# Key places by chunk, shared query places, and later planned sums in a scheduled attention and FNet kernel

## The chip, the cores and the metric

The kernel runs on one core of a Trainium2 chip. Five engines work beside each other: TensorE (matmuls), VectorE (DVE), ScalarE (ACT), GpSimd (POOL) and SyncE (SP), which in this kernel issues every DMA. Each engine takes its instructions strictly in the order in which the program has them. The metric is the device time of one execution in microseconds, the median of several runs.

## The reference

Two independent halves are computed in float32, and written side by side into an output of 2048 x 896.

```python
# A: Fourier mixing, x of 2048 x 448
a = einsum("bsd,ed->bse", x, dft_hid_re); b = einsum("bsd,ed->bse", x, dft_hid_im)
y = einsum("ts,bse->bte", dft_seq_re, a) - einsum("ts,bse->bte", dft_seq_im, b)
# B: softmax attention, 16 heads of width 28 over 2048 tokens
q, k, v = split(x @ wqkv)
p = softmax(q k^T * 28 ** -0.5)
out = (p v) @ wo
```

The inputs of B are multiplied by 8, so that the scores are large and the softmax needs its row maxima.

## The kernel before, in words

**Accuracy.** Products that need more than one pass are split into a high and a low part ("hi", "lo"): three passes for the products of `products`, and for the scores 84 rows of a key or query tile (28 of one part twice, 28 of the other).

**Half A and the projections** are "filling" work for TensorE: the projection of queries, keys and values (L547), the hidden transform (`hidden`, also L547), and the transform along the sequence (`sequence`, L662, 1536 matmuls of 448 columns). Their weights come through three buffers "wraw" (DMA at L515), are rounded by ScalarE (L516), and POOL takes the rest (L522). Query and key parts are written to a DRAM tensor "qkd" and loaded from there, per head and chunk.

**Attention** is cut into units of one head and one chunk of 512 queries, 64 in all, in two lanes. A "kept" unit (`unit_kept`, 48 of them) scores once: 16 matmuls (L803) with keys as rows, copies kept in SBUF (L415), a running maximum on VectorE (L810, L813), the maximum turned and spread by transposes (L820, L822, L829, L831), then the shift on POOL or VectorE (L846), the exponential on ScalarE (L850), and the product with the values (L734). A "twice" unit (`unit_twice`, 16) scores once for the maxima alone (L753, L757), sends the 4 x 128 maxima through DRAM into two more rows of its query tile (L765 to L770, tensor "nmd"), and scores again with these rows (L781), so that ScalarE's exponential (L785) reads the shifted scores at once. Each head has one twice unit, mostly the chunk 1.

**The sums** (`out_of`, L854 to L884): once per head (per chunk for the last two heads) TensorE folds the four partial results (L865), ScalarE copies them (L867), a DMA gathers the rows of sums into a small tile "sm" (L870), VectorE inverts them (L871), they go to DRAM (L872, "rd") and come back spread over 32 partitions (L876), POOL multiplies (L879), and the result is stored (L882). At the end the output projection loads it again (L939, L944), splits it into halves hi and lo that stand in a key tile (L956, L411), and multiplies by wo (L974).

**What sets the order.** Nothing is ordered by hand. All work is given to a planner (`Schedule`) as tasks, each with an engine, a key (when it is due), an estimated duration, dependencies, and the buffer places that it uses. The planner plays through an estimated course: whenever an engine is free, it takes the ready task with the smallest key for which places are free, and emits it. So the estimates fix each engine's order once and for all; on the chip an engine that comes to an instruction whose input is late waits, and everything behind it on that engine waits too. For a DMA the estimate is the size, plus the `extra` microseconds given in the call, and SP is taken as busy for 0.38 us per DMA.

**Places.** A pool of places (`Slots`) gives them out when a task that uses one is emitted, and takes one back when its last user is done. With `in_turn` a place goes only to the earliest due takers. A head's keys are one place of 128 x 2048, of two (`kt_s`); `head_loads` fills it with four chunk loads of two DMAs each (L689, L690), due one microsecond after the other. Twice units take one of two query places "qr", kept units one of two "qk".

Of the kernel before, what the change touches and what calls it, by code (L numbers as in the profile page):

```python
# [20 lines left out]
S = 2048  # L21
D = 448
H = 16
DH = 28
# [10 lines left out]
LATE = 110.0  # L35
NFILL = 2
# [280 lines left out]
def tile_kernel(ctx, tc, xa, wre, wim, wd, xb, wqkv, wo, out):  # L317
# [381 lines left out]
    def head_loads(h):  # L699
        k = KT[h] = kt_s.slot()  # L700
        for c in range(NC):
            got_k[h, c] = [dma(head_due[h] - 14 + c, lambda c=c: rows_of(
                k.t[:, c * CH:(c + 1) * CH], 1, h * 2 * DH + DH, c * CH, (c + 1) * CH),
                size=84, extra=X_ROWS, n=2, deps=rows_ready(h, c, DH), use=[k])]
        v = VT[h] = v_s.slot()
        got_v[h] = [dma(head_due_b[h] - 12, lambda: nc.sync.dma_start(
            v.t.rearrange("p c t d -> p (c t d)"), v_d[h]), deps=[d for c in range(NC) for d in v_done[c]], use=[v])]
# [34 lines left out]
    def unit_twice(u):  # L742
        h, c = u
        t_a, t_b, dt = due[u]
        q = qr_s.slot()
# [3 lines left out]
        for kc in range(NC):  # L749
            for qt in range(4):  # L750
                o = bank_s.slot()
                key = t_a + (kc * 4 + qt) * dt
                m = pe(key, lambda e, o=o, kc=kc, qt=qt: nc.tensor.matmul(  # L753
                    o.t, q.t[:KR, qt * P:(qt + 1) * P], KT[h].t[:KR, kc * CH:(kc + 1) * CH], start=True, stop=True),
                    deps=[*lq, *got_k[h, kc], before.get("ra")], use=[o, q, KT[h], mx])
# [17 lines left out]
        for g in range(NT // GV):  # L773
            tiles, es = [], []
            for kt in range(GV * g, GV * (g + 1)):
                o = bank_s.slot()
                if kt % 2 == 0:
                    tiles.append(kept_s.slot())
                p = Half(tiles[-1], kt % 2)
                key = t_b + kt * dt  # L780
                m = pe(key, lambda e, o=o, kt=kt: nc.tensor.matmul(  # L781
                    o.t, KT[h].t[:KR + 2, kt * P:(kt + 1) * P], q.t[:KR + 2, :], start=True, stop=True),
                    deps=[ld, before.get("rb")], use=[o, p.pair, q, KT[h], po])
                in_line("rb", m)
                es.append(act(key - 20, lambda o=o, p=p: nc.scalar.activation(p.t, o.t, AF.Exp, scale=SCALE),  # L785
                              deps=[m], use=[o, p.pair]))
            last_pv = pv_group(u, g, tiles, [*es, last_pv], po, key)
        unit_out(u, po, last_pv, key - 20)

    def unit_kept(u):  # L790
        h, c = u
        t_a, t_b, dt = due[u]
        q = qk_s.slot()
# [3 lines left out]
        for kt in range(NT):  # L797
            o = bank_s.slot()
            if kt % 2 == 0:
# [4 lines left out]
                o.t, KT[h].t[:KR, kt * P:(kt + 1) * P], q.t[:KR, :], start=True, stop=True),  # L804
                deps=[*lq, *got_k[h, kt // 4], before.get("ka")], use=[o, s.pair, rm, q, KT[h]])
# [50 lines left out]
    def out_of(us, rd):  # L856
# [13 lines left out]
        s2 = dma(key, lambda: nc.sync.dma_start(sm.t[:, :n * NC], osb.t[DH:n * VW:VW, :]), 8, 0.7, deps=[a], use=[sm, pair])  # L870
        r = dve(key - 20, lambda: nc.vector.reciprocal(sm.t[:, :n * NC], sm.t[:, :n * NC]), 0.3, deps=[s2], use=[sm])  # L871
        s3 = dma(key, lambda: nc.sync.dma_start(rd, sm.t[:, :n * NC]), 8, deps=[r], use=[sm])  # L872
# [5 lines left out]
        s4 = dma(key, spread, 64, n=n, deps=[s3], use=[pair])  # L878
# [52 lines left out]
    for n, c in enumerate(LAST):  # L931
# [15 lines left out]
        for i in range(2):  # L947
            x = kt_s.slot()
            ready = []
            for k in range(4):  # L950
                raw, ld = raws[k]
                src = lambda raw=raw, i=i: raw.t[:, i * HF:(i + 1) * HF]
                hi = lambda x=x, k=k: x.t[:, k * HF:(k + 1) * HF]
                lo = lambda x=x, k=k: x.t[:, (4 + k) * HF:(5 + k) * HF]
                key = T_OUT + n + i / 2
                a = act(key, lambda hi=hi, src=src: nc.scalar.activation(hi(), src(), AF.Copy), 0.3, deps=[ld], use=[raw.pair, x])  # L956
                if k < 3:
                    b = sub(key, lo, src, lambda hi=hi: f32(hi()), d=0.35 if OUT_DVE else 0.65, early=OUT_DVE, deps=[a], use=[raw.pair, x])
                else:
                    b = sub(key, lambda hi=hi: hi()[64:], lambda src=src: src()[64:], lambda hi=hi: f32(hi())[64:], d=0.35 if OUT_DVE else 0.65, early=OUT_DVE,  # L960
                            deps=[a], use=[raw.pair, x])
                ready += [a, b]
            for t in range(2):
                o = bank_s.slot()

                def cols(k, x=x, t=t):
                    return lambda: x.t[:, k * HF + t * P:k * HF + (t + 1) * P]
# [7 lines left out]
                m = pe(key, emit, n=11, d=M448, deps=[*ready, *wo_ready], use=[o, x])  # L975
# [44 lines left out]
```

## Time and profile before

| what | value |
|---|---|
| runs (3) | 1185.16, 1185.59 and 1194.47 us, median 1185.59 |
| profiled execution, own time | 1186.24 us |
| its span, first to last instruction | 1184.5 us |
| mean granted clock of TensorE | 0.997 |
| busy: ACT | 89% |
| busy: DVE | 79% |
| DMA, mean rate over the span | 106 GB/s |

The span is the time between the first and the last instruction in the trace; the execution's own time has 1.7 us around it. "Busy" counts computing instructions of an engine. The trace also tells, for each idle piece of an engine, which other engine or DMA ended it ("<-"), and the chain of waits follows the end of the program back from releaser to releaser. "SPq" is SP's queue: what it shows as a duration is the issue of a DMA, not its transfer.

### The profile page before, as it was taken

How to read it: one execution, taken by the hardware profiler on the slowest of the kernel's cores; microseconds unless marked ns; L12 is line 12 of the kernel's file. 1: busy time of each engine (PE TensorE's matmuls, PEld its weight loads, DVE VectorE, ACT ScalarE, POOL GpSimd, SP SyncE). 2: the span in 40 equal slices, each digit the busy share in tenths (PEclk: the TensorE clock that was granted, in tenths of full speed). 3: DMA queues.
4: the chain of work that ended last, by engine and by line, in shares of the span. 5: the costliest groups of instructions: out<-in, count | busy, mean ns of one | idle time of the engine just before them, and what ended most of it. 6: DMA issues, size and time to landing. Idle time of an engine off the chain costs nothing.

```text
span 1184.5 us, 19835 instructions
## 1 busy us (share of the span) xinstructions
PE 1164.1 (98%) x6426; PEld 809.4 (68%) x6426; DVE 936.7 (79%) x1468; ACT 1056.5 (89%) x1777; POOL 909.9 (77%) x525
## 2 busy tenths in 40 slices
PE   8999999999999999999999999999999999999998
PEld 7876656666667666766666667666667676667677
DVE  6599988888888868877787888987877888877742
ACT  5279999999999989998899999999999999999942
POOL 1157868989888979877797989897987897997730
PEclk9999999999999999999999999999999999999999
DMA  7792235322323232323132232323232423223643
GB/s 244 165 225 107 100 124 174 90 81 62 106 68 110 62 109 67 105 72 90 62 102 89 78 118 67 106 64 111 83 99 89 121 76 115 87 62 100 188 130 119
DMA packets 111736, 125.18 MB, mean 106 GB/s; under 512 B 49264, under 2 KB 63216, under 8 KB 111632
## 3 DMA queue, kind: packets, MB, share of 16 engines
q1 hardware_dynamic: 111632, 123.91, 35.4%
q8 instruction: 51, 0.84, 0.3%
q14 instruction: 53, 0.43, 0.1%
HBM read 89.98 MB, written 33.75 MB: 104 GB/s over the span
## 4 chain that ended last, share of the span: by engine, by line
PE 82%; ACT 6%; DMA 4%; DVE 2%; issue 2%; POOL 2%; SPq 1%; ACTq 0%; POOLq 0%; DVEq 0%
PE bank L662 23%; PE bank L734 17%; PE bank L803 14%; PE bank L547 11%; PE bank L781 5%; PE bank L753 5%; PE bank L974 3%; ACT kept L415 3%; PE bank L820 2%; PE bank L829 2%; DVE rm L813 2%; ACT kept L850 1%; PE bank L865 1%; DMA kept<-xb 1%; POOL kept L846 1%
## 5 line engine op out<-in xcount | busy, mean ns | idle before, releaser
L846 POOL TENSOR_TENSOR kept<-kept,mb 128x1024 f32<-128x1024 f32 x263 | 626.9, 2404 | 124.0 <-ACT mb L831 101.4
L813 DVE TENSOR_TENSOR rm<-bank,rm 128x512 f32<-128x512 f32 x672 | 461.1, 686 | 74.9 <-ACT kept L415 33.5
L415 ACT ACTIVATE kept<-bank 128x512 f32<-128x512 f32 (+1 forms) x715 | 408.5, 633 | 53.9 <-PE bank L803 34.6
L850 ACT ACTIVATE kept<-kept 128x1024 f32<-128x1024 f32 x372 | 395.1, 1102 | 11.3 <-DVE kept L846 5.5
L662 PE MATMUL bank<-big,whi 128*128 128x448 f32 x1024 | 328.6, 370 | 0.0
L803 PE MATMUL bank<-qk,k 84*128 84x512 f32 x768 | 292.0, 410 | 2.7 <-ACT kept L415 1.4
L522 POOL TENSOR_TENSOR wlo<-wraw,whi 128x512 fp32r<-128x512 f32 (+1 forms) x166 | 204.0, 1232 | 70.3 <-ACT whi L516 46.7
L734 PE MATMUL bank<-kept,v 128*32 128x512 f32 x1988 | 240.7, 597 | 0.7 <-DVE rm L813 0.5
L662 PEld LDWEIGHTS bank<-big,whi 128*128 128x128 f32 x1024 | 193.7, 190 | 28.8 <-issue 3.5
L803 PEld LDWEIGHTS bank<-qk,k 84*128 84x128 f32 x768 | 141.9, 189 | 69.3 <-DVE rm L813 17.7
L662 PE MATMUL bank<-big,wlo 128*128 128x448 f32 x512 | 189.0, 369 | 0.0
L757 DVE TENSOR_REDUCE mx<-bank 128x1 f32<-128x512 f32 x256 | 173.3, 682 | 18.8 <-PE bank L753 18.0
L785 ACT ACTIVATE kept<-bank 128x512 f32<-128x512 f32 x250 | 157.6, 639 | 5.3 <-PE bank L781 5.0
L734 PEld LDWEIGHTS bank<-kept,v 128*32 128x32 f32 x1988 | 56.6, 109 | 124.0 <-issue 111.9
L846 DVE TENSOR_TENSOR kept<-kept,bank 128x1024 f32<-128x1024 f32 x109 | 131.8, 1212 | 2.6 <-ACT mb L831 2.4
L516 ACT ACTIVATE whi<-wraw 128x512 fp32r<-128x512 f32 x167 | 112.1, 673 | 17.0 <-DMA wraw<-wqkv 12.2
L781 PE MATMUL bank<-qr,k 86*128 86x512 f32 x256 | 104.3, 411 | 2.9 <-DMA qr<-nmd 2.2
L662 PEld LDWEIGHTS bank<-big,wlo 128*128 128x128 f32 x512 | 97.2, 190 | 13.7 <-issue 0.8
L753 PE MATMUL bank<-k,qr 84*128 84x512 f32 x256 | 103.5, 413 | 2.3 <-ACT kept L785 0.9
L547 PE MATMUL bank<-wd,whi 128*128 128x448 f32 x256 | 80.6, 368 | 0.1
L547 PE MATMUL bank<-big,whi 128*128 128x512 f32 x196 | 69.8, 400 | 2.0 <-ACT big L482 0.9
L822 DVE TENSOR_REDUCE nm<-bank 128x4 f32<-128x512 f32 x48 | 33.1, 690 | 46.5 <-PE bank L820 43.4
(80 smaller groups left out, 1062.0 us busy)
## 6 DMA issues: line engine op xcount, KB each, us to landing
wraw<-wre SPq DMA_DIRECT2D x64, 256.0 KB
wraw<-wim SPq DMA_DIRECT2D x64, 256.0 KB
qkd<-wd SPq DMA_DIRECT2D x32, 256.0 KB
wraw<-xa SPq DMA_DIRECT2D x32, 256.0 KB
k<-qkd SPq DMA_DIRECT2D x64, 112.0 KB
out<-kept SPq DMA_DIRECT2D x32, 224.0 KB
qkd<-kept SPq DMA_DIRECT2D x24, 256.0 KB
qk<-qkd SPq DMA_DIRECT2D x48, 112.0 KB
```

Of the source, the lines that this page charges most:

```text
L415: nc.scalar.activation(dst, src, AF.Copy)
L522: b = sch.add(e, at, lambda g: eng[g].tensor_tensor(self.lo.t[:, :n], raw.t[:, :n], f32(self.hi.t)[:, :n], op=ALU.subtract), deps=[a], acq ...
L547: nc.tensor.matmul(o.t[:, :cols], w(), x(), start=(i == 0), stop=(i == n - 1))
L662: nc.tensor.matmul(o.t[:, :D], a.t[:, k, :], b[:, q * 4 + k, :], start=(q == 0 and k == 0 and j == 0), stop=(q == 3 and k == 3 and j == 2))
L734: nc.tensor.matmul(o.t[j * VW:(j + 1) * VW, :], VT[h].t[:, kt // 4, j, :], pairs[i // 2].t[:, i % 2, :], start=(kt < 4), stop=(kt >= NT - 4))
L753: m = pe(key, lambda e, o=o, kc=kc, qt=qt: nc.tensor.matmul(o.t, q.t[:KR, qt * P:(qt + 1) * P], KT[h].t[:KR, kc * CH:(kc + 1) * CH], start ...
L757: ms.append(dve(key - 20, lambda o=o, kc=kc, qt=qt: nc.vector.tensor_reduce(mx.t[:, qt, kc:kc + 1], o.t, axis=AX.X, op=ALU.max), deps=[m], ...
L781: m = pe(key, lambda e, o=o, kt=kt: nc.tensor.matmul(o.t, KT[h].t[:KR + 2, kt * P:(kt + 1) * P], q.t[:KR + 2, :], start=True, stop=True), ...
L803: m = pe(key, lambda e, o=o, kt=kt: nc.tensor.matmul(o.t, KT[h].t[:KR, kt * P:(kt + 1) * P], q.t[:KR, :], start=True, stop=True), deps=[*l ...
L813: prev = dve(key - 20, lambda o=o: nc.vector.tensor_tensor(rm.t, o.t, rm.t, op=ALU.max), deps=[m, prev], use=[rm, o], lock=[o], own=RAW)
L846: eng[e].tensor_tensor(s.t, s.t, over_pair(pm.t if e == "DVE" else mb.t), op=ALU.add)
L850: es.append(act(key, lambda s=s: nc.scalar.activation(s.t, s.t, AF.Exp, scale=SCALE), 0.96, deps=[sh], use=[s]))
```

## The change

Three things are changed.

1. A head's keys are no longer one tile of 128 x 2048 of two, but four tiles of 128 x 512 of eight (`NKEYS = 8`); the memory is the same. Each chunk's tile is taken by its own load and given back after its own last matmul. The matmuls read the chunk's tile. The output projection takes four such tiles for its halves where it took one large tile.
2. The two pools of two query places become one pool of four, given out in the order of need to both lanes.
3. In `out_of` the planner's estimate of three DMAs rises: the gathering of the sums by 3.0 instead of 0.7 us, the store of the reciprocals and their spreading by 1.5 us each instead of nothing. No instruction changes through this; the planner puts what depends on them later.

```diff
+NKEYS = 8
-    kt_s = new("k", [P, S], F32R, 2, True)
+    kt_s = new("k", [P, CH], F32R, NKEYS, True)
-    qk_s = new("qk", [P, CH], F32R, 2, True)
-    qr_s = new("qr", [P, CH], F32R, 2, True)
+    q_s = new("q", [P, CH], F32R, 4, True)
...
     def head_loads(h):
-        k = KT[h] = kt_s.slot()
+        KT[h] = [kt_s.slot() for c in range(NC)]
         for c in range(NC):
-            got_k[h, c] = [dma(head_due[h] - 14 + c, lambda c=c: rows_of(
-                k.t[:, c * CH:(c + 1) * CH], 1, h * 2 * DH + DH, c * CH, (c + 1) * CH),
+            k = KT[h][c]
+            got_k[h, c] = [dma(head_due[h] - 14 + c, lambda k=k, c=c: rows_of(
+                k.t, 1, h * 2 * DH + DH, c * CH, (c + 1) * CH),
                 size=84, extra=X_ROWS, n=2, deps=rows_ready(h, c, DH), use=[k])]
...
-                    o.t, KT[h].t[:KR, kt * P:(kt + 1) * P], q.t[:KR, :], start=True, stop=True),
-                deps=[*lq, *got_k[h, kt // 4], before.get("ka")], use=[o, s.pair, rm, q, KT[h]])
+                    o.t, KT[h][kt // 4].t[:KR, kt % 4 * P:(kt % 4 + 1) * P], q.t[:KR, :], start=True, stop=True),
+                deps=[*lq, *got_k[h, kt // 4], before.get("ka")], use=[o, s.pair, rm, q, KT[h][kt // 4]])
...
-        s2 = dma(key, lambda: nc.sync.dma_start(sm.t[:, :n * NC], osb.t[DH:n * VW:VW, :]), 8, 0.7, deps=[a], use=[sm, pair])
+        s2 = dma(key, lambda: nc.sync.dma_start(sm.t[:, :n * NC], osb.t[DH:n * VW:VW, :]), 8, 3.0, deps=[a], use=[sm, pair])
...
-        s3 = dma(key, lambda: nc.sync.dma_start(rd, sm.t[:, :n * NC]), 8, deps=[r], use=[sm])
+        s3 = dma(key, lambda: nc.sync.dma_start(rd, sm.t[:, :n * NC]), 8, 1.5, deps=[r], use=[sm])
...
-        s4 = dma(key, spread, 64, n=n, deps=[s3], use=[pair])
+        s4 = dma(key, spread, 64, 1.5, n=n, deps=[s3], use=[pair])
...
-            x = kt_s.slot()
+            x = [kt_s.slot() for _ in range(4)]
...
+                xh, xl = x[k // 2], x[2 + k // 2]
```

The same replacement of `KT[h]` by the chunk's tile stands in the two scoring passes of `unit_twice`, and `q_s.slot()` in both unit functions. At the start POOL fills rows 64 to 95 of every key tile with ones (L374); these are now eight tiles.

More of the change, by code (lines that the diff above doesn't have):

```diff
@@ L744, in unit_twice @@
         t_a, t_b, dt = due[u]
-        q = qr_s.slot()
+        q = q_s.slot()
         lq = load_q(u, q)
@@ L781, in unit_twice @@
                 m = pe(key, lambda e, o=o, kt=kt: nc.tensor.matmul(
-                    o.t, KT[h].t[:KR + 2, kt * P:(kt + 1) * P], q.t[:KR + 2, :], start=True, stop=True),
-                    deps=[ld, before.get("rb")], use=[o, p.pair, q, KT[h], po])
+                    o.t, KT[h][kt // 4].t[:KR + 2, kt % 4 * P:(kt % 4 + 1) * P], q.t[:KR + 2, :], start=True, stop=True),
+                    deps=[ld, before.get("rb")], use=[o, p.pair, q, KT[h][kt // 4], po])
                 in_line("rb", m)
@@ L792, in unit_kept @@
         t_a, t_b, dt = due[u]
-        q = qk_s.slot()
+        q = q_s.slot()
         lq = load_q(u, q)
@@ L974, in emit @@
                         nc.tensor.matmul(o.t[:, :D], x(), w(), start=(n == 0), stop=(n == 10))
-                m = pe(key, emit, n=11, d=M448, deps=[*ready, *wo_ready], use=[o, x])
+                m = pe(key, emit, n=11, d=M448, deps=[*ready, *wo_ready], use=[o, *x])
                 pair = kept_s.slot()
```

16 lines of the change are left out of this document (8 added, 8 removed).

## The prediction

> **What bounds the kernel now.** I read the page's first two parts for the bounding engine, then the waits of TensorE alone, then the chain of waits around each of them, and last the SP queue's timeline at the worst one.
>
> ```profile
> span 1184.5 us, 19835 instructions
> PE 1164.1 (98%) x6426; PEld 809.4 (68%) x6426; DVE 936.7 (79%) x1468; ACT 1056.5 (89%) x1777; POOL 909.9 (77%) x525
> ```
>
> TensorE is busy for 1164.1 of 1184.5 us, so its idle time is 20.4 us. A change that adds and removes no matmul can win little more than this, and only the part that it touches.
>
> ```profile
> PE bank L781 <- DMA qr<-nmd: 2.2, 3, 0.8
> PE bank L829 <- DVE nm L822: 1.9, 1, 1.9
> PE bank L803 <- ACT kept L415: 1.4, 1, 1.4
> PE bank L753 <- ACT kept L785: 0.9, 1, 0.9
> PE bank L803 <- ACT ou L415: 0.8, 1, 0.8
> PE bank L753 <- DVE rm L813: 0.7, 1, 0.7
> PE bank L781 <- DVE rm L810: 0.6, 1, 0.6
> PE bank L753 <- DMA qr<-qkd: 0.6, 1, 0.6
> PE bank L734 <- DVE rm L813: 0.5, 1, 0.5
> PE bank L803 <- ACT kept L785: 0.2, 1, 0.2
> ```
>
> These are TensorE's own waits in the attention part (total us, times, longest), ten rows with 9.8 us in all; the rest of its idle time lies at the start, where both programs have the same order, at the end, and in pieces too short for this view. The chain of waits shows what stands ahead of most of them:
>
> ```profile
> 172.30 2.30 DMA sm<-kept
> 416.14 1.43 DMA qr<-nmd
> 422.06 4.30 DMA sm<-kept
> 552.50 2.54 DMA sm<-kept
> 624.94 2.17 DMA kept<-rd
> 681.85 2.91 DMA wraw<-wd
> 932.22 1.46 DMA qr<-nmd
> ```
>
> "sm" and "rd" belong to a head's sums and reciprocals (out_of), "nmd" to the row maxima of the twice lane (the first and the last of three such waits), "wraw" to a weight load. All are small or single transfers on the SP queue. What stands ahead of them there is shown by the SP timeline at the worst place:
>
> ```profile
> 548.26 0.60 ACT L867 ACTIVATE kept<-bank 128x512 f32<-128x512 f32 x1 [0.30 <-PE bank L865]
> 546.78 0.80 SPq L689 DMA_DIRECT2D k<-qkd  x1
> 547.62 0.54 SPq L690 DMA_DIRECT2D k<-qkd  x1
> ...
> 552.05 0.35 SPq L706 DMA_DIRECT2D v<-vd  x1
> 552.50 0.61 SPq L870 DMA_DIRECT2D sm<-kept  x1
> 555.07 0.25 DVE L871 RECIPROCAL sm<-sm 128x16 f32<-128x16 f32 x1 [4.13 <-DMA sm<-kept]
> ```
>
> The first row is ScalarE's copy of the sums, ready at 548.9. A head's whole key tile comes free at once, so its four chunks (0.80 + 0.54 us of issue each), a query load and the values go out in one burst from 546.8 to 552.4. The sums' transfer L870 stands behind it. VectorE has the reciprocal next in its order and idles for 4.13 us; TensorE waits 0.6 (L753, for the query load in the burst) and 1.9 us (L829, for the maximum behind the reciprocal). The order of SP in the program has such a burst at every head: between two chunk loads of one head stand mostly 0 or 2 other issues, and L870 or L769 follows. The same burst delays the maxima at the three places and the weight load at 681.85.
>
> ```profile
> 553.60:557.20 3.60, 1.69 (x10) 1.03 (x9) 2.13 (x5) 0.59 (x2) 0.00 (x0) 1.00 0.39 117
> 557.20:560.60 3.40, 3.40 (x11) 2.89 (x10) 3.20 (x5) 3.07 (x6) 2.39 (x1) 0.50 0.47 137
> ```
>
> These windows show that the granted clock (the column behind POOL) is 0.50 for the 3.4 us after this wait. At half clock that stretch does 1.7 us of work, so 1.7 us more are lost.
>
> **The change, part by part.**
>
> *Work.* The two built orders hold the same matmuls: 5329 TensorE instructions in each, and 220 switches between 32-column and full-width matmuls in each. The first 679 stand in the same order. So TensorE's busy time stays, and the prediction is a matter of its waits.
>
> *Keys in eight places.* Chunk loads stay 128 DMAs of the same size. In the new SP order, however, 4 to 8 other rows stand between two chunk loads of a head, so the burst is gone. One chunk (1.4 us of issue) can still stand ahead of L870 or L769. This takes away the three waits on nmd (2.2), the wait on the query load (0.6) and the one that follows the weight load at 681.85 (L753 behind L785, 0.9): 3.7 us. New is that each chunk load waits for its own place on SP; behind it stand weight loads. I bound this in the rivals.
>
> *Queries in four shared places.* No instruction changes. The twice lane's first scoring pass now begins earlier: the TensorE work between the end of one first pass and the start of the next falls from about 13 to about 6 us in most units. The second passes stay within 7 us of where they were. I cost it at nothing, because TensorE always has filling matmuls (L662) to put there. If that cover were gone, one late query would cost as the row above, 0.6 us.
>
> *Sums planned later.* The three edits (3.0 for 0.7, 1.5, 1.5) change planned landing times alone. By adding up TensorE's durations along the order, with these rows,
>
> ```profile
> 492.94 1.85 PE bank L734 x16
> 495.45 0.47 PE bank L803 x2
> 1172.06 9.01 PE bank L974 x44
> ```
>
> (0.235 for 512 columns, 0.205 for 448, 0.116 for a 32-column one), I place the reciprocal on VectorE by the TensorE work between the fold and the score that VectorE handles just before it. Over the first 16 groups that is 2.4 us in the mean before and 3.6 us after. What it needs is shown where nothing stood in the way:
>
> ```profile
> 947.33 0.60 ACT L867 ACTIVATE kept<-bank 128x512 f32<-128x512 f32 x1 [1.12 <-PE bank L865]
> 950.28 0.24 DVE L871 RECIPROCAL sm<-sm 128x16 f32<-128x16 f32 x1
> ```
>
> That is 3.0 us from the fold's end, which released the copy. Before, 13 of 16 reciprocals are closer than that; after, 2. With two short issues ahead of it on SP, like L706 above (0.35 each), the need is 3.7: 15 are closer before, 8 after. The waits that follow a sum are L829 (1.9), L753 behind L813 at 426 (0.7), L781 behind L810 at 176 (0.6) and L803 behind "ou" at 632 (0.8): 4.0 us, and the half clock, 1.7 us: 5.7 us. They are at most all gone and at least all back; I keep a third of them, 1.9 us, between 2/13 and 8/15 by the counts just given. What is late next is the multiplication L879 on POOL, 6 us later in the plan. POOL is 77% busy and TensorE waits for no L879, so it costs nothing until the tail:
>
> ```profile
> 1152.10 1.39 POOL L879 TENSOR_TENSOR kept<-kept 64x512 f32<-64x512 f32 x1 [8.92 <-DMA kept<-rd]
> ```
>
> The last multiplication ends at 1153.5 and the last four output groups start at 1172.06, 18.6 us later, with a store, a reload and the splitting between. Were it 6 us later, 12.6 us would be left for these; without that cover the 6 us would be paid in full, 1185.
>
> *Rows of ones and the output's halves.* Eight memsets of 32x512 replace two of 32x2048:
>
> ```profile
> L374 POOL MEMSET k<- 32x2048 f32 x2 | 3.5, 1798 | 0.1
> L506 POOL MEMSET wd<- 64x448 f32 x4 | 1.9, 466 | 0.2
> ```
>
> By the second row 8 x 0.47 = 3.7 us, for 3.6. A weight piece's memset stands behind them, which may come 0.2 us later; I take zero. In the output projection four small key places replace one large one, with the same copies.
>
> *The clock.* The half clock came after idle pieces of 0.6 and 1.9 us, none longer. The Trainium skill (TensorE: Matmul & The Clock Gate, the table "Why this matters for your kernels") asks for no idle gap over about 3 us and sees the half clock after one such window. By that rule the drop would not be this wait's doing and would stay, and the sum would be 1.1 us higher, 1179.8; the trace speaks against it here.
>
> *Sum.* 3.7 + 5.7 - 1.9 = 7.5 us less than the profiled execution's 1186.24 us (span 1184.5 and 1.7 around it): 1178.7, about 1179. The median of the runs, 1185.59, is 0.65 below the profiled one, which is less than the terms are sure of; I keep 1179, 0.6% below the median.
>
> **The rivals.** One per cent (11.9 us) is about what a measurement of this kernel can tell from no change.
>
> (a) New waits take the place of the old. Every planned order of so many units has its own tight spots, and the waits of 1.4, 0.5 and 0.2 us that I left in are such. If they come back for all that goes, the time is 1186. For it: the attention part already loses only 9.8 us. Against it: the burst is one cause for several waits, and it is visibly gone.
>
> (b) The burst is not the cause, since issue is short beside a transfer. Then only the sums' terms are won: 5.7 - 1.9 = 3.8, 1182.4. Against it: L870 was issued at 552.50, 3.6 us after its source was ready, while the transfer took 2.5. The Trainium skill (DMA: Bandwidth & Descriptors, "Issuing engines are not separate DMA queues") calls the time to initiate a DMA usually small relative to the DMA; in these rows it is not.
>
> (c) Slower: SP stands before a key place that is not yet free, with weight loads behind it.
>
> ```profile
> SPq L515 <- POOL wlo L522: 235.8, 77, 13.5
> SPq L689 <- PE bank L803: 54.8, 19, 8.3
> ```
>
> Such a wait is 2.9 us in the mean (second row). After the first eight places 56 chunks must each wait for a place, where 14 heads did. If each starves TensorE once by 0.73 us (2.2 in 3), all 56 cost 41 us: 1220. It decides from (11.9 + 7.5)/0.73 = 27 of them; I take 1200 for this rival. Against it: SP waits 235.8 us for a weight place to come free, so it has time in hand almost everywhere.
>
> (d) All of it goes: the ten waits (9.8) and the clock (1.7), 1186.24 - 11.5 = 1174.7. For it: with the SP burst gone, and each unit's scores begun earlier, no row names a cause that must remain. Against it: 8 of 16 reciprocals are still close.
>
> **How the numbers follow.** My forecast, a gain of 0.3 to 0.9%, has 0.47; (a) 0.17, (b) 0.10, (c) 0.06, (d) 0.20. The time is 1179. The range reaches down to (d), less the 1.1 us by which the profiled run and the fastest one (1185.16) differ, and up just past (a): 1173.5 to 1187. (d) lies 1.0 us above the bound of 1%, 1173.7, so half of it, 0.10, counts as faster by over 1%; slower is (c), 0.06; the rest, 0.84, is within 1%.
>
> **What would show it.** TensorE's waits on "nmd" and on a query load gone or halved; no DVE idle before L872 (L871 now) over 1 us, where 4.13 stood; no stretch of half clock after 50 us; SP's chunk loads apart from each other. Wrong it would be if TensorE's waits again add up to 10 us in the attention part under other names, or if SP's waits before key loads grow and weights come late.

## The result and the profile after

| what | before | after |
|---|---|---|
| median of the runs (6 and 6) | 1185.38 us | 1168.82 us |
| lowest and highest | 1183.68, 1194.47 | 1167.11, 1172.55 |
| ratio with its 95% interval | | 0.9848 [0.9811, 0.9885] |
| profiled execution, own time | 1186.24 us | 1167.41 us |

The change makes the kernel faster by 1.5%, 16.6 us between the medians. The prediction had 1179, a gain of 0.6%, and its range ended at 1173.5: the direction was right, the size was not half of what came, and the time lies below the range.

First the page's head and its chain of work, of the kernel after:

```profile
span 1165.6 us, 19879 instructions
PE 1155.8 (99%) x6426; PEld 810.0 (69%) x6426; DVE 934.8 (80%) x1473; ACT 1054.0 (90%) x1773; POOL 908.1 (78%) x530
...
PE 94%; DVE 2%; POOL 1%; issue 1%; ACT 1%; DMA 1%; SPq 0%; DVEq 0%; ACTq 0%
```

TensorE's idle time falls from 20.4 us to 9.8 (1165.6 - 1155.8). That is 10.6 of the span's 18.9; the other 8.3 us stand within what the page calls busy. The waits of TensorE after, all rows that the view gives (us in total, times, longest):

```profile
PE bank L821 <- DVE rm L814: 2.1, 1, 2.1
PE bank L892 <- POOL ident masks.py:199: 1.4, 1, 1.4
PE bank L547 <- DVE kept L589: 1.3, 2, 1.1
PE bank L547 <- DVE big L411: 1.1, 1, 1.1
PE bank L782 <- DVE rm L814: 0.2, 1, 0.2
```

The rows of L892 and L547 lie at the start. In the attention part ten rows with 9.8 us have become two with 2.3 us (from L697 on a line is one further down than before, so L782 is the L781 of before). No row names a transfer any more. The same stretch as the one shown before around 552, in the kernel after, ScalarE's copy of the sums, SP and VectorE alone:

```profile
540.36 0.35 SPq L707 DMA_DIRECT2D v<-vd  x1
540.90 0.36 SPq L515 DMA_DIRECT2D wraw<-wre  x1
541.87 0.60 ACT L868 ACTIVATE kept<-bank 128x512 f32<-128x512 f32 x1 [0.94 <-PE bank L866]
542.49 0.61 SPq L871 DMA_DIRECT2D sm<-kept  x1
...
547.43 0.24 DVE L872 RECIPROCAL sm<-sm 128x16 f32<-128x16 f32 x1
```

The transfer is issued 0.02 us after the copy's end (542.47), where it was 3.6 us late, and VectorE comes to the reciprocal 5.0 us after the copy without idling. Over the first 16 groups of sums the lateness of this issue adds up to 11.7 us before and 0.8 after.

POOL's wait ahead of the multiplication with the reciprocals, before and then after:

```profile
POOL kept L879 <- DMA kept<-rd: 23.1, 9, 8.9
```
```profile
POOL kept L880 <- DMA kept<-rd: 5.7, 7, 1.1
```

These rows hold only the waits that the view puts down to the transfer of the reciprocals. Whoever is named, POOL idled for 37.7 us ahead of its 18 multiplications before, and for 8.3 us after.

**Where the 18.9 us of the span went.** TensorE's matmuls and transposes start at fixed distances when nothing hinders them (0.236 us after a scoring matmul, 0.205 after one of 448 columns, and so on). What a start is later than that is lost, also where no idle time is shown because the instruction before seems to take longer. Up to the 400th TensorE instruction both programs have the same order; after it I sort the losses by length.

| loss of TensorE, us | before | after | less |
|---|---|---|---|
| start of the 400th instruction | 94.0 | 90.2 | 3.8 |
| after it: losses over 0.2 us (18 and 2 of them) | 13.6 | 2.6 | 11.0 |
| losses of 0.05 to 0.2 us | 23.1 | 20.4 | 2.7 |
| still shorter ones | | | 0.9 |
| at half clock | 1.5 | 1.5 | 0.0 |
| the rest | | | 0.5 |

The first line is no work of the change: over all kernels below with the same order up to there it lies between 89.7 and 98.1. The half clock has not gone, it has moved. The windows around TensorE's one long wait after (time, then busy time of PE, PEld, DVE, ACT and POOL, the granted clock, DMA share and GB/s):

```profile
276.00:280.00 4.00, 1.91 (x13) 0.97 (x15) 3.75 (x8) 4.00 (x8) 4.00 (x3) 1.00 0.14 45
280.00:283.60 3.60, 3.60 (x19) 0.95 (x12) 0.75 (x2) 3.25 (x5) 3.44 (x4) 0.53 0.01 2
```

VectorE is busy for 3.75 of 4.00 us ahead of that: here the maxima of a unit are late because VectorE itself is full, not because it waits.

### The profile page after: what moved, and what is told of

Same layout as the page of the kernel before. It is cut to its first block, busy times and chain, and to the rows that moved or that the text cites. A ratio compares the mean times of both kernels' runs of the same rounds, so it can differ in the third digit from the quotient of the medians.

```text
span 1165.6 us, 19879 instructions
## 1 busy us (share of the span) xinstructions
PE 1155.8 (99%) x6426; PEld 810.0 (69%) x6426; DVE 934.8 (80%) x1473; ACT 1054.0 (90%) x1773; POOL 908.1 (78%) x530
## 4 chain that ended last, share of the span: by engine, by line
PE 94%; DVE 2%; POOL 1%; issue 1%; ACT 1%; DMA 1%; SPq 0%; DVEq 0%; ACTq 0%
PE bank L662 27%; PE bank L735 19%; PE bank L804 15%; PE bank L547 13%; PE bank L782 5%; PE bank L754 5%; PE bank L976 3%; PE bank L821 2%; PE bank L830 2%; PE bank L866 1%; DVE rm L814 1%; POOL kept L847 1%; DMA kept<-wqkv 0%; DVE big L411 0%; ACT kept L415 0%
## 5 line engine op out<-in xcount | busy, mean ns | idle before, releaser
L415 ACT ACTIVATE kept<-bank 128x512 f32<-128x512 f32 (+1 forms) x711 | 410.2, 634 | 55.7 <-PE bank L804 31.9
L662 PE MATMUL bank<-big,whi 128*128 128x448 f32 x1024 | 324.5, 369 | 0.0
L804 PE MATMUL bank<-q,k 84*128 84x512 f32 x768 | 290.2, 408 | 0.2
L804 PEld LDWEIGHTS bank<-q,k 84*128 84x128 f32 x768 | 141.8, 189 | 63.7 <-DVE rm L814 14.7
L786 ACT ACTIVATE kept<-bank 128x512 f32<-128x512 f32 x250 | 159.6, 643 | 3.6 <-PE bank L782 3.4
L754 PE MATMUL bank<-k,q 84*128 84x512 f32 x256 | 104.7, 410 | 0.0
L782 PE MATMUL bank<-q,k 86*128 86x512 f32 x256 | 104.2, 410 | 0.2 <-DVE rm L814 0.2
L547 PE MATMUL bank<-wd,whi 128*128 128x448 f32 x256 | 80.1, 368 | 0.0
L547 PE MATMUL bank<-big,whi 128*128 128x512 f32 x196 | 70.0, 400 | 1.4 <-DVE big L411 1.1
```

What stands on the lines that cost most here:

```text
L415: nc.scalar.activation(dst, src, AF.Copy)
L547: nc.tensor.matmul(o.t[:, :cols], w(), x(), start=(i == 0), stop=(i == n - 1))
L662: nc.tensor.matmul(o.t[:, :D], a.t[:, k, :], b[:, q * 4 + k, :], start=(q == 0 and k == 0 and j == 0), stop=(q == 3 and k == 3 and j == 2))
L754: m = pe(key, lambda e, o=o, kc=kc, qt=qt: nc.tensor.matmul(o.t, q.t[:KR, qt * P:(qt + 1) * P], KT[h][kc].t[:KR, :], start=True, stop=True ...
L782: m = pe(key, lambda e, o=o, kt=kt: nc.tensor.matmul(o.t, KT[h][kt // 4].t[:KR + 2, kt % 4 * P:(kt % 4 + 1) * P], q.t[:KR + 2, :], start=T ...
L804: m = pe(key, lambda e, o=o, kt=kt: nc.tensor.matmul(o.t, KT[h][kt // 4].t[:KR, kt % 4 * P:(kt % 4 + 1) * P], q.t[:KR, :], start=True, sto ...
```

## The experiments

What had to be told apart: **theory 1**, the prediction's, that the burst of a head's key loads on SP delays small transfers, and that later planned sums take the rest of their waits away; **theory 2**, that the shared query places, which I had costed at nothing, bring what the sum missed; **theory 3**, that any new planned order draws its own few waits, so that much of the difference is luck. Each ratio is against runs of the kernel before on the same chip; its medians there lay between 1184.0 and 1187.7 us.

### The three parts alone

**Key places alone:** eight key places by chunk; two pools of two query places and the old estimates stay.

```diff
+NKEYS = 8
-    kt_s = new("k", [P, S], F32R, 2, True)
+    kt_s = new("k", [P, CH], F32R, NKEYS, True)
```

> The kernel before with the key places alone: eight places of one chunk, two query pools as before, sums planned as before. Theory 1 (the burst of key loads on SP): most of the gain is here; the order of SP has 3 to 13 other rows between the chunk loads of a head. The waits on nmd (2.2 us), on the query load (0.6) and behind the weight load (0.9) go, and of the waits behind the reciprocals the part that the burst caused: 1174 to 1178 us, TensorE's own waits in the attention part 3 to 5 us. Theory 2 (the shared query places give the slack): nearly nothing, 1183 to 1186. Theory 3 (every new order has its own luck): any time between 1175 and 1195, with about ten waits of 0.5 to 2 us at other places. For the first 50 us: if the 3.3 us won there belong to the key places or their memsets, they show here too.

Measured: 1176.4 us, ratio 0.9927 [0.991, 0.9945]. The issue of the sums, late by 11.7 us over the first 16 groups before, is late by 0.9, and no TensorE wait on "nmd" or on a query is left. SP at the same head (lines stand one or two further down than in the kernel before):

```profile
541.26 0.82 SPq L690 DMA_DIRECT2D k<-qkd  x1
542.13 0.54 SPq L691 DMA_DIRECT2D k<-qkd  x1
542.77 0.36 SPq L708 DMA_DIRECT2D v<-vd  x1
543.76 0.60 ACT L869 ACTIVATE kept<-bank 128x512 f32<-128x512 f32 x1 [0.27 <-PE bank L867]
544.38 0.61 SPq L872 DMA_DIRECT2D sm<-kept  x1
...
546.75 0.24 DVE L873 RECIPROCAL sm<-sm 128x16 f32<-128x16 f32 x1
```

One chunk, not four, stands ahead of the copy, and the transfer leaves 0.02 us after it. Nothing was planned later here: the reciprocal comes 2.4 us after the copy.

**Query places alone:**

```diff
-    qk_s = new("qk", [P, CH], F32R, 2, True)
-    qr_s = new("qr", [P, CH], F32R, 2, True)
+    q_s = new("q", [P, CH], F32R, 4, True)
```

> The kernel before with the four shared query places alone. The burst stays (0 to 2 other rows between the chunk loads). Theory 1: 1184 to 1188, the waits on nmd and behind reciprocals as before, about 10 us. Theory 2: 1170 to 1177, since the first scoring pass of the twice lane can begin earlier. Theory 3: anything between 1175 and 1195.

Measured: 1182.49 us, 0.998 [0.9966, 0.9995]. The burst stays (the sums' issue is late by 13.3 us in all). Two in a thousand is not what the sum missed; by themselves the query places are not the main cause.

**Sums planned later, alone:** the three estimates, nothing else.

```diff
-..., osb.t[DH:n * VW:VW, :]), 8, 0.7, deps=[a], ...)
+..., osb.t[DH:n * VW:VW, :]), 8, 3.0, deps=[a], ...)
-        s3 = dma(key, lambda: ..., 8, deps=[r], use=[sm])
-        s4 = dma(key, spread, 64, n=n, deps=[s3], use=[pair])
+        s3 = dma(key, lambda: ..., 8, 1.5, deps=[r], use=[sm])
+        s4 = dma(key, spread, 64, 1.5, n=n, deps=[s3], use=[pair])
```

> The kernel before with the later planned sums alone; key and query places as before. The burst stays. Theory 1: the waits behind reciprocals (4.0 us) and the half clock that follows one (1.7) go, the waits on nmd and on the query load stay: 1180 to 1183. Theory 2: 1184 to 1187. Theory 3: anything between 1175 and 1195.

Measured: 1173.2 us, 0.9902 [0.9882, 0.9922]. The smallest edit gives the most. The burst is still there in its trace, at the same head:

```profile
545.49 0.80 SPq L689 DMA_DIRECT2D k<-qkd  x1
545.63 0.60 ACT L867 ACTIVATE kept<-bank 128x512 f32<-128x512 f32 x1 [0.49 <-PE bank L865]
546.33 0.55 SPq L690 DMA_DIRECT2D k<-qkd  x1
546.93 0.37 SPq L706 DMA_DIRECT2D v<-vd  x1
547.40 0.37 SPq L515 DMA_DIRECT2D wraw<-wre  x1
547.87 0.60 SPq L870 DMA_DIRECT2D sm<-kept  x1
...
551.48 0.24 DVE L871 RECIPROCAL sm<-sm 128x16 f32<-128x16 f32 x1
```

The transfer is late by 1.6 us (547.87 against 546.23) and nobody minds: VectorE comes to the reciprocal 5.2 us after the copy, as late as it needs. VectorE's idling before reciprocals falls from 7.2 to 2.6 us over the kernel, POOL's before the multiplications from 37.7 to 16.4, whoever ended it.

### Two parts together, and parts of the sums

**Keys and queries, old estimates:**

```diff
-..., 8, 3.0, deps=[a], ...)
+..., 8, 0.7, deps=[a], ...)
-        s3 = dma(key, lambda: ..., 8, 1.5, deps=[r], use=[sm])
-        s4 = dma(key, spread, 64, 1.5, n=n, deps=[s3], use=[pair])
+        s3 = dma(key, lambda: ..., 8, deps=[r], use=[sm])
+        s4 = dma(key, spread, 64, n=n, deps=[s3], use=[pair])
```

> The changed kernel with the sums planned as before. Theory 1: as the key places alone, 1173 to 1178, with some waits of VectorE for the reciprocals left (2 to 4 us). Theory 2: as the changed kernel or within 2 us of it, 1168 to 1171. Theory 3: between 1165 and 1185, not tied to the parts.

Measured: 1179.15 us, 0.9951 [0.9933, 0.9969]: by the median slower than the keys alone, though the intervals overlap, with waits of 2.4 and 2.5 us of its own. The first of these stands at 182.6, behind ScalarE, which waited for POOL, which had waited for the reciprocals:

```profile
179.76 1.29 POOL L880 TENSOR_TENSOR kept<-kept 128x512 f32<-128x512 f32 x1 [3.43 <-DMA kept<-rd]
181.02 7.07 POOL L847 TENSOR_TENSOR kept<-kept,mb 128x1024 f32<-128x1024 f32 x3
183.43 1.06 ACT L851 ACTIVATE kept<-kept 128x1024 f32<-128x1024 f32 x1 [2.59 <-POOL kept L847]
184.40 0.58 ACT L786 ACTIVATE kept<-bank 128x512 f32<-128x512 f32 x1
...
185.03 0.74 PE L804 MATMUL bank<-q,k 84*128 84x512 f32 x2 [2.42 <-ACT kept L786]
```

The waits view files this under L786, an instruction that has nothing to do with the sums. It made me doubt the "costs nothing" of the multiplication. The expectations call it **theory 4** that POOL's waits before the multiplications cost time, and **theory 5** that only VectorE's waits before the reciprocals do.

**Keys and later sums, separate query pools:**

```diff
-    q_s = new("q", [P, CH], F32R, 4, True)
+    qk_s = new("qk", [P, CH], F32R, 2, True)
+    qr_s = new("qr", [P, CH], F32R, 2, True)
```

> The changed kernel without its shared query places (two pools of two, as before). The parts measured alone gave 0.9927 (keys), 0.9902 (sums) and 0.998 (queries). Theory 1 (keys clear SP, sums clear VectorE and POOL, queries carry nothing): as the changed kernel, 1166 to 1171, with no idle time of VectorE before a reciprocal and less than 10 us of POOL's before the 18 multiplications. Theory 2 (the query places are needed for the last part of the gain): 1173 to 1177, as the better of the two parts.

Measured: 1179.54 us, 0.995 [0.9931, 0.9968], a miss. No reciprocal is waited for, and POOL idles for 9.7 us before its multiplications, as theory 1 had said; the time is not what it had said. Its profiled execution, 1182.21 us, has a loss at 81 that no planned wait explains: one store of a projection took SP 2.19 us to issue where most take 0.3 to 0.4, and VectorE's next subtraction needed its place:

```profile
80.06 0.69 SPq L594 DMA_DIRECT2D qkd<-wd  x1
80.86 2.19 SPq L593 DMA_DIRECT2D qkd<-wd  x1
...
83.84 0.69 DVE L590 TENSOR_TENSOR wd<-bank,wd 128x512 fp32r<-128x512 f32 x1 [3.95 <-DMA qkd<-wd]
...
85.18 0.29 PEld L755 LDWEIGHTS bank<-k,qr 84*128 84x128 f32 x1 [3.67 <-DVE rm L815]
```

A stretch of 6.4 us at half clock follows (granted 0.50), 3.2 us more. This execution's span is 14.8 us longer than that of the kernel after, and 7.9 of these lie before the 400th TensorE instruction (98.1 against 90.2 us), where both have the same order: that part is not the order's. Whether the other five had it too is not recorded. The six runs lie from 1175.97 to 1182.21, so this profile is the slowest of them; but even the fastest is above the 1166 to 1171 that theory 1 had for it. The combination differs from the kernel after by its query pools alone, and it is 0.8 to 1.0% slower, clear of both intervals. Why it is slower than that, and than the sums alone, stays open.

**Keys with only the store and the spreading planned later** (1.5 and 1.5; the gathering at its old 0.7), and **keys with only the gathering planned later** (3.0; the others at their old value):

```diff
-        s3 = dma(key, lambda: ..., 8, deps=[r], use=[sm])
-        s4 = dma(key, spread, 64, n=n, deps=[s3], use=[pair])
+        s3 = dma(key, lambda: ..., 8, 1.5, deps=[r], use=[sm])
+        s4 = dma(key, spread, 64, 1.5, n=n, deps=[s3], use=[pair])
```

> Key places, and of the sums' estimates only the two behind the reciprocal (1.5 us for the store of the reciprocals, 1.5 for the spreading); the gathering of the sums is planned as before, 0.7. With the key places alone VectorE's idle time before reciprocals is already gone (0.6 us in 16) while POOL still idles some 25 us before the multiplications. Theory 4 (what the sums' estimates bring on top of the keys is POOL's idle time): 1169 to 1172, POOL's idle time before multiplications under 12 us. Theory 5 (it is the reciprocal's place on VectorE): as the keys alone, 1175 to 1178.

```diff
-..., osb.t[DH:n * VW:VW, :]), 8, 0.7, deps=[a], ...)
+..., osb.t[DH:n * VW:VW, :]), 8, 3.0, deps=[a], ...)
```

> Key places, and of the sums' estimates only the first (3.0 us for the gathering of the sums); store and spreading as before. Theory 4 (POOL): POOL idles about as with the keys alone, 15 to 25 us before the 18 multiplications, and the time stays at 1174 to 1177. Theory 5 (VectorE): 1168 to 1171.

Measured: 1170.11 us, 0.9877 [0.986, 0.9894], and 1173.15 us, 0.9894 [0.9878, 0.991]. Either half of the estimates, on top of the keys, gives nearly all; the half that moves POOL's multiplication, not VectorE's reciprocal, is no worse. In it POOL idles for 5.5 us before the multiplications, where the keys alone had 29.1, and the time is where theory 4 had put it. With the gathering alone POOL still idles for 19.3 us, and the time lies between what the two theories had said. Neither kernel has shared query places.

**The order shaken:** the kernel after, with one planned duration changed by 0.1 ns.

```diff
-    M512, M448, MS = 0.2335, 0.2065, 0.2365
+    M512, M448, MS = 0.2335, 0.2065, 0.2366
```

> The changed kernel with one estimate of the planner shifted by 0.0001 us (a score matmul 0.2366 for 0.2365), which changes no work and no place, only the order in which close decisions fall. Theory 3 (every order has its own luck): the time moves by more than 4 us to either side of 1168.8. Theories 1 and 4: it stays within 2.5 us of it, 1166.3 to 1171.3, with no idle time before reciprocals. The first 50 us have the same order as in the changed kernel; if their 3.3 us belong to the change, matmul number 150 starts within 0.5 us of 37.9, and if they belong to the run, anywhere between 37.5 and 42.

Measured: 1171.81 us, 0.9889 [0.9871, 0.9906]. A tick of a planner's number that means nothing goes with a ratio 0.2 to 0.4% above those of the kernel after (0.9848, and 0.9869 in the next run), some 2 to 5 us; the intervals overlap, so it may be less. That lies between what theory 3 (over 4 us) and theories 1 and 4 (within 2.5 us) had said. At this size theory 3 can't be ruled out: what differs by 0.2 or 0.3% between two orders is not to be explained by their parts.

**The kernel after once more,** unedited, beside the kernels of the next part:

> The changed kernel once more, unedited. Its order of TensorE is the same as before's up to instruction 679, yet its profile was 3.3 us ahead at matmul 150, and other kernels with the same order stood between 3.9 us ahead and 1.1 behind. If these 3.3 us belong to the run and not to the change, matmul 150 comes anywhere between 37.4 and 42.3 us here, and the median lies between 1168 and 1172; if they belong to the change, at 37.9 within 0.3.

Measured: 1168.61 us, 0.9869 [0.9855, 0.9883]. The two measurements of the change place its gain at 1.3 and 1.5%, and their intervals reach from 1.2 to 1.9%.

### The waits of the sums by themselves

These edits keep the kernel before with every instruction in its place, and leave out only that an engine needs the sums or their reciprocals; their results are not normalized.

**POOL multiplies by nothing that is late.** The results are multiplied by themselves in place of the reciprocals; all DMAs still go out.

```diff
-        mul = pool(key - 20, lambda: nc.gpsimd.tensor_tensor(osb.t[:n * VW], osb.t[:n * VW], sbc.t[:n * VW], op=ALU.mult),
+        mul = pool(key - 20, lambda: nc.gpsimd.tensor_tensor(osb.t[:n * VW], osb.t[:n * VW], osb.t[:n * VW], op=ALU.mult),
```

> The kernel before, every engine's order unchanged, but the multiplication of L879 multiplies the results with themselves and not with the spread reciprocals, so that POOL no longer waits for their transfer (the normalization is left out of the result). Theory 4 (POOL's idle time before the multiplications, 37.7 us in 18, costs TensorE through the shifts and weight parts behind it): 1177 to 1181 us. Theory 5 (only VectorE's wait for the sums costs): 1184 to 1186.

Measured: 1180.39 us, 0.9969 [0.9955, 0.9982], where theory 4 had put it. What the prediction had put at nothing costs 0.31%, 3.7 us. (The multiplication itself is shorter here too, 1.03 us for 1.30, 4.7 us in 18; the idle time that went is 37.7.) In the kernel before it worked like this at 632 (the rows of one chain, in the order in which they follow):

```profile
627.26 1.30 POOL L879 TENSOR_TENSOR kept<-kept 128x512 f32<-128x512 f32 x1 [2.43 <-PE bank L803]
628.53 1.28 POOL L522 TENSOR_TENSOR wlo<-wraw,whi 128x512 fp32r<-128x512 f32 x1
629.77 2.40 POOL L846 TENSOR_TENSOR kept<-kept,mb 128x1024 f32<-128x1024 f32 x1
...
632.20 1.06 ACT L850 ACTIVATE kept<-kept 128x1024 f32<-128x1024 f32 x1 [1.37 <-POOL kept L846]
...
633.80 0.50 PE L803 MATMUL bank<-qk,k 84*128 84x512 f32 x1 [0.82 <-ACT ou L415]
```

POOL idles 2.43 us before the multiplication. The row puts this down to TensorE, but the chain of waits has the transfer of the reciprocals there (from 624.94, 2.17 us, the row "kept<-rd" of the prediction), which ends 0.15 us before the multiplication starts. The shift behind it (L846) comes late, ScalarE idles 1.37 us for that, and its next copies, which free TensorE's banks, come late too. Without the need for the reciprocals this wait of TensorE and the one of 1.4 us at 508 (L803 behind L415) are gone. Ahead of that second one POOL had idled 2.43 us before the multiplication at 495, and then had work without a break until the shift that ended at 508.35. Of TensorE's waits in the attention part that are left, the largest are

```profile
PE bank L829 <- DVE nm L822: 1.7, 1, 1.7
PE bank L781 <- DMA qr<-nmd: 1.6, 3, 0.6
```

**VectorE inverts nothing that is late.** First try: it copies from a constant tile, and the sums go to a spare DRAM tensor.

```diff
-        r = dve(key - 20, lambda: nc.vector.reciprocal(sm.t[:, :n * NC], sm.t[:, :n * NC]), ...)
+        r = dve(key - 20, lambda: nc.vector.tensor_copy(sm.t[:, :n * NC], ident[:, :n * NC]), ...)
```

> The kernel before, every engine's order unchanged, but L871 copies a constant instead of inverting the sums, and the gathering DMA writes to a DRAM scratch, so that VectorE no longer waits for it (the reciprocals are left out of the result). POOL still waits for the rest of the round trip, and what the burst delays there. Theory 5, and the sum in the prediction (5.7 us with the half clock): 1179 to 1182. Theory 4: 1182 to 1185.

Measured: 1218.16 us, 1.0291 [1.0267, 1.0314], slower. The same with the multiplication by itself as well:

> Both edits together, order unchanged: neither VectorE nor POOL waits for the sums' round trip (the normalization is left out of the result). What is left of the ten waits of TensorE are those on nmd, on the query load and behind the weight load, which the burst causes, 3.7 us idle. If the two kinds of wait add up: 1172 to 1176. If one covers the other: as the better of the two alone.

Measured: 1215.7 us, 1.0272 [1.0253, 1.0291]. The edit brought a cost of its own. Its rows, groups first, then one copy and POOL beside it:

```profile
L872 DVE COPY sm<-ident 128x16 f32<-128x16 f32 (+1 forms) x18 | 32.2, 1788 | 0.0
```
```profile
356.60 9.51 POOL L847 TENSOR_TENSOR kept<-kept,mb 128x1024 f32<-128x1024 f32 x4 [0.66 <-ACT mb L832]
...
365.19 4.48 DVE L872 COPY sm<-ident 128x16 f32<-128x16 f32 x1
366.06 1.28 POOL L523 TENSOR_TENSOR wlo<-wraw,whi 128x512 fp32r<-128x512 f32 x1
367.29 2.35 POOL L847 TENSOR_TENSOR kept<-kept,mb 128x1024 f32<-128x1024 f32 x1
```

The copy of 128 x 16 takes 4.48 us and ends at 369.67, POOL's third instruction at 369.64. Here it was held as long as POOL had work. Of the 18 copies of the first kernel the shortest took 0.16 us, the mean is 1.8 and the longest 5.0. The reciprocal of the same shape takes 0.24 us in the mean. The Trainium skill (SBUF — State Buffer, "SBUF: two separate sides") says that VectorE, in some of its operations, and GpSimd share a pair of ports as an exclusive lock, held for a whole instruction, and that the other blocks. The trace agrees, and shows more: the copy lost to three POOL instructions in a row. These two kernels tell nothing of the reciprocal's wait.

Second try: the reciprocal stays a reciprocal, but of the tile with the row maxima, which is never late; the sums go to the spare tensor again.

```diff
+        r = dve(key - 20, lambda: nc.vector.reciprocal(sm.t[:, :n * NC], mx_s.tiles[0]...[:, :n * NC]), ...)
```

> As the kernel without VectorE's wait for the sums, but L871 inverts the twice lane's maxima, which VectorE itself wrote, in place of a copy of a constant: that copy took up to 5.0 us (1.7 in the median, the reciprocal 0.24) while POOL was busy, and so measured itself. Every engine's order is that of the kernel before; the normalization is left out of the result. By the prediction's sum (5.7 us with the half clock, of which a third kept): 1180 to 1182. Theory 5 (VectorE's wait is what costs): 1176 to 1181. Theory 4 (POOL's wait costs): 1182 to 1185.

Measured: 1182.48 us, 0.9965 [0.9949, 0.9981]: the wait before the reciprocals costs 0.35%, 4.2 us. Both needs taken away:

> VectorE inverts the maxima and POOL multiplies the results with themselves, order unchanged, the normalization left out of the result: nothing waits for the sums' round trip any more, while the burst of key loads stays. POOL's part alone gave 0.9969. If the waits add up: 1172 to 1177, and what is left are the waits on nmd and the query load. If later planned sums alone (0.9902) had their gain from these waits, this kernel must come near them: 1172 to 1176.

Measured: 1176.93 us, 0.9919 [0.9898, 0.994], 0.81% or 9.6 us: somewhat more than 0.31 and 0.35, within the intervals. That is near the 0.98% of the later planned sums alone, again within the intervals, as it must be if their gain came from these waits. With the burst still on SP four waits for "nmd" remain, 2.2 us (L782 is the L781 of before):

```profile
PE bank L782 <- DMA qr<-nmd: 2.2, 4, 0.9
```

And key places alone together with both:

> The key places alone (0.9927), and in that order neither VectorE nor POOL waits for the sums' round trip (the normalization left out of the result). It has no burst, no wait for sums, and neither the later plan nor the shared query places. If burst and sums' waits are the whole cause: 1167 to 1171, as the changed kernel. If the order that the later plan makes matters by itself: 1173 to 1176.

Measured: 1173.49 us, 0.9894 [0.9871, 0.9917]. A kernel with no burst and without any wait for a sum gains 1.1%, by these two mechanisms alone. Between this and the change's 1.3 to 1.5% lie some 3 to 5 us. The time is in the second of the two ranges expected, the one for an order that matters by itself; but the intervals overlap, and the shaken order moved about as far, so these runs do not decide it.

**Still later:** the kernel after with the spreading planned at 4.0 in place of 1.5.

```diff
-        s4 = dma(key, spread, 64, 1.5, n=n, deps=[s3], use=[pair])
+        s4 = dma(key, spread, 64, 4.0, n=n, deps=[s3], use=[pair])
```

> The changed kernel with the spreading of the reciprocals planned another 2.5 us later (4.0 for 1.5), so that POOL's remaining 6 to 8 us of idle time before the multiplications go. If that idle time still costs: 1165 to 1167. If it is covered: within 2.5 us of 1168.7.

Measured: 1171.42 us, 0.9872 [0.9847, 0.9897]. POOL still idles 9.0 us before its multiplications in all (8.3 in the kernel after), so the edit did not take away what it was meant to, and whether these last 8 us cost anything is not shown. No version ran clearly faster than the kernel after.

## Why the prediction was right in direction and wrong in size

**The burst on SP: right.** Key places by chunk take it away, and with it the waits on "nmd", on the query and behind the weight load that I had listed; the keys alone bring 0.73%, 8.7 us, where I had 3.7. The difference is that the burst also fed the waits that I had filed under the sums: without it a transfer leaves at most 0.4 us after the copy in place of up to 3.6, so even the old, too short plan holds more often. Where nothing waits for a sum any more, the key places bring 0.25% (from 0.9919 to 0.9894, with intervals that overlap), 3.0 us: near the 3.7 of my sum.

**The two terms were not separate.** A sum is late by what SP adds and needed too early by what the plan leaves out. Either remedy brings half of the gain or more: 0.73% by the keys, 0.98% by the estimates, 1.3 to 1.5% by all. So "the burst is one cause for several waits" was half the truth; with the estimates alone the burst stands and two of the three waits on "nmd" are gone.

**"TensorE waits for no L879, so it costs nothing until the tail": the step that failed.** It costs 3.7 us, of which my sum held only the 0.8 us of one wait. POOL idled 37.7 us before its multiplications, 23.1 of them in nine waits that the view puts down to the reciprocals, and what stands behind the multiplication on POOL is a shift that ScalarE needs, whose copies free TensorE's banks. TensorE's row names only the last of that chain ("ou", L415). Of the waits on L803 I had given the 0.8 us to the reciprocals and left the 1.4 us in as none of theirs; both were POOL's. The chain that I showed had named it, "kept<-rd" at 624.94, and I counted the wait without asking who had waited for that transfer. That the plan puts the multiplication 6 us later did cost nothing; it took away a wait that my step had not seen.

**"I keep a third of them, 1.9 us": wrong.** No reciprocal in the kernel after is waited for; all 18 start without idle time. I had placed them 3.6 us behind the fold in the mean, adding up TensorE's durations along the order. On the chip the first 16 come 4.4 to 5.7 us behind the copy's end, so 5.0 and more behind the fold: VectorE, 80% busy, runs behind TensorE, and this lag is added to the distance in the order.

**Sizes by the waits view: too small.** Ten rows gave 9.8 us; by the distance between starts the long losses after the common part are 13.6 us, 11.0 of them gone, and 3.6 more in short ones. Each wait costs some 0.15 to 0.25 us more than its idle piece (at 553.65, before, 2.07 us between starts for 1.91 idle), and six more losses of 0.2 to 0.3 us had no row. 3.8 us of the profiled pair are run-to-run variation of the start, no gain.

**The half clock, 1.7 us: wrong.** It moved from 557 to 280, behind a wait that VectorE's own load causes.

**Queries at nothing: right alone, open in combination.** They bring 0.2% [0.05, 0.34] alone. Put on top of the keys they go with 0.24% more time, within the noise; put on top of keys and later sums, with 0.8 to 1.0% less, which is more than the shaken order moved. Since keys with either half of the estimates come to 0.9877 and 0.9894 without them, they are not needed for most of the gain; what they do in the whole change stays open.

**The rivals.** Of mine (d), that all of it goes, was the nearest, and it too was high at 1174.7, since its 9.8 us were the idle view's. (c), SP stuck before key places, did not come: SP waits longer at L689, which issues the loads of keys and of queries (before, the largest such row had 54.8 us), in two rows of its queue after

```profile
SPq L515 <- POOL wlo L522: 176.5, 71, 8.0
SPq L689 <- PE bank L804: 73.6, 25, 7.1
SPq L689 <- PE bank L662: 60.3, 26, 8.3
```

but it has that time: its wait for a weight place fell from 235.8 us to 176.5, and TensorE waits for no weight.

**What stays open:** the last 3 to 5 us between both mechanisms by themselves and the change, which may be noise or the order's own; why keys with later sums but separate query pools are slower than the change and than the later sums alone.

## What to carry to other kernels

Where engines run a fixed order, look for every engine that waits for a transfer, also one that is far from the bound, and ask what stands behind the waiting instruction and who needs that: the bounding engine's row will carry another name. A round trip through DRAM that a plan takes too short is dear at each of its steps and can be mended by the estimate alone, before any buffer is changed. Before the parts of a change are told apart by tenths of a per cent, shake the order with a meaningless tick, and see how much that moves. One tick gives only a sample: here one combination of the same parts lay further off than the tick had moved.

## What the runs showed of the hardware that I had not expected

- The half clock is not set by a wait's length alone. It followed waits of 2.1 us in the kernel after and in its shaken version, one of 1.9 us with the queries alone, and even one of 1.3 us, with 0.45 us more just behind it, in the kernel with key places and neither wait (half clock from 718.9), but not the waits of 2.4 and 2.5 us of keys with queries. The windows of keys with queries at 182 (columns as above) show a fuller pause, and the full clock behind it:

```profile
182.00:185.00 3.00, 0.60 (x3) 0.18 (x1) 1.10 (x2) 1.57 (x3) 3.00 (x2) 1.00 0.77 273
185.00:189.00 4.00, 3.97 (x17) 3.26 (x18) 3.30 (x6) 3.71 (x6) 4.00 (x3) 1.00 0.58 202
```

  The Trainium skill (TensorE: Matmul & The Clock Gate, "Why this matters for your kernels") asks for no gaps over about 3 us; by these runs 2 us can already be too long, and need not be.

  Where a wait lies in time seems to matter. In every trace the changes of the granted clock lie whole multiples of 3.41 us apart. On that grid the wait of the kernel after falls into one piece (276.7 to 280.1, TensorE busy for 1.31 us of it), and half clock begins with the next; the 2.4 us wait of keys with queries crosses an edge (at 184.4), with 1.70 and 2.77 us busy in the two pieces. This is no full rule: a piece with 1.46 us busy (keys with later sums, from 1125.8) was followed by full clock, one with 2.05 (the second kernel without VectorE's wait, from 177.8) by half.
- A tiny VectorE copy between SBUF tiles was held up to 5.0 us by POOL in the one kernel that had it and up to 6.0 in the other; a reciprocal of the same shape never took more than 0.26 us.
- Issue on SP is not one price: 0.82 us for the first DMA of a key chunk and 0.54 for the second, 0.34 and 0.38 for the two of a query load (medians of the kernel after). And every trace has 5 to 10 issues of 1.5 us and more, 4 to 6 of them in the first 75 us, for DMAs that mostly take 0.3 to 0.9: the 2.19 us at 81 above is one of these, and the kernel after has a store with 2.21 at 26.4.
- The start of the kernel, in the same order, reached its 400th TensorE instruction between 89.7 and 98.1 us.
